# Linear attention and a gated mixture of experts on one core: batch 3's x^T by DMA transposes, 17 more zero matmuls, and another written order

## The chip, the cores and the metric

The kernel runs on one core of a Trainium2 chip. The metric is the device time of one execution in microseconds (us). Five engines work beside each other, each with its own instruction queue: PE (TensorE, matrix products), ACT (ScalarE, activations), DVE (VectorE, elementwise work), POOL (GpSimd) and SP (SyncE, which here only issues DMA transfers). Every engine takes its instructions strictly in the order in which they were written. An instruction that waits therefore holds up everything written behind it on its engine. The transfers themselves run on 16 DMA engines that all queues share.

## The reference

For 8 batches of 8 heads, with 576 tokens and a head dimension of 64, the kernel computes linear attention and then, with the 8 heads laid side by side (512 channels), one expert per token.

```python
phi = lambda x: np.where(x > 0, x, np.exp(x) - 1.0) + 1.0
kv = einsum('bhsd,bhse->bhde', phi(k), v);  z = sum(phi(k), axis=2)
x = einsum('bhsd,bhde->bhse', phi(q), kv) / (einsum('bhsd,bhd->bhs', phi(q), z)[..., None] + 1e-06)
...
logits = x @ w_gate;  local = sigmoid(x @ w_local)
# per token: the expert of the largest logit if local < 0.5 (or it is the first token), else the expert before
out[b, s] = p[e] * (relu(x[b, s] @ w1[e]) @ w2[e])
```

Here p is the softmax of the logits, w1 is 8 x 512 x 1024 and w2 is 8 x 1024 x 512.

## The kernel before, in words

The kernel assumes that one expert serves a whole batch, the one of its first token. It computes that case and a flag that says whether it held; only if it did not, a general branch follows (it isn't entered with these inputs).

The work is cut into 803 named steps. The list `ops` (lines 660 to 817) says for each step which engine takes it, what it needs, and which PSUM slot it takes or gives back. There are four PSUM slots of two banks each. `TURNS` (lines 92 to 131) is a permutation of the 803 steps, and the instructions are emitted in exactly that order; so it fixes the order on every engine and every DMA queue. The costs and latencies in `ops` are what a planner outside the kernel worked with; inside the kernel only the needs and the slots count. `fills` (line 88) says how many matmuls of zeros (`work`, line 825) PE does just ahead of a named step.

In the text n counts half batches (four heads each, 0 to 15), a counts batches (0 to 7), j = n mod 2, and h counts the two halves of a batch's first 512 tokens. The steps are:

- **Loads, SP queue.** Lk.n, Lv.n, Lq.n bring k, v and q of a half batch (`load`, `load_wide`, lines 154 to 196). Lk.n and Lv.n from n = 2 on are three DMA instructions each (L167 once, L170 twice), Lq.n is one (L159). There are 4 buffers for k, 3 for v and 2 for q, so Lk.n needs K.(n-4), Lv.n needs VC.(n-3), and Lq.n needs the DVE step P.q.(n-2). HOLD (line 542) is a tiny transfer that makes the loads of batches 2 to 7 wait until batch 0's w1 has landed. Lwg brings the gate weights.
- **phi, ACT and DVE.** E (exp, L279) and E2 (relu, L285) run on ACT, P.k.n (L307) and P.q.n (L314, two instructions) on DVE. VC.n copies v beside a column of ones (L326).
- **Attention, PE.** K.n accumulates kv (L337, L342; L349 for batch 0), KC.n copies it out (DVE, L354). Q.n and QL.a transpose phi(q) (L360, L374), QC.n and QLC.a copy that out (ACT, L366, L380). N.a.j.h and NL.a are the numerators and denominators (L401, L420); D.a.j.h and DL.a divide (DVE, L386, L388, L389) and write x in bf16 into `xb` (one buffer for each h, reused by every batch).
- **x transposed.** XL.a and XLC.a do the last 64 tokens on PE and DVE (L453, L457). For the other 512 tokens there are two ways. For batches a < TB, X.a.h is 8 PE transposes (`x_main`, L435) and XC.a.h a DVE copy (`x_main_out`, L440). For the others, X.a.h is two DMA transposes on the SP queue (`x_dma`, line 444, L447), 128 x 512 bf16 each, and XC.a.h stands for their landing.
- **Gate.** R.a.0 and R.a.1 are the logits (L468, L474), PK.a picks the expert of the first token (DVE), W.a.x issues the load of that expert's w1 or w2 on the POOL queue (L533, L536, L538; skipped by a condition if one of three slots holds it), CW.a.x copies it into the working buffer (DVE, L552). S1, S2, S3 make the gate's factor.
- **Experts.** H.a.m (m = 0 to 7) are 8 matmuls each for the hidden layer (L590); HC.a.m is the relu on ACT (L597). O.a.i (i = 0 to 4; O0 is the first part of O.a.0) is the output layer (L609, L613); OC.a.i scales it on ACT (L623, L625), and ST.a.* stores it (SP queue).

A need that matters below: D.a.j.h overwrites `xb`, so it needs the transposes of batch a-1 to have read it. In line 734 that is X.(a-1).h while a <= TB, and the landing XC.(a-1).h for a > TB. H.a.0 needs XC.a.0, XC.a.1, XLC.a and the expert's weights.

Of the kernel before, what the change touches and what calls it, by code (L numbers as in the profile page):

```python
# [48 lines left out]
def kernel(  # L49
# [28 lines left out]
    W = Dh + 1  # L78
    rows = [P, P, P, P, PH]
    LEAD = 2  # L80
    TB = 4
    NS = 3
    NX = 3
    BOTH = "kq"
    SLOTS = [2, 2, 2, 2]


    fills = {("FILL",): 19, ("QL", 0): 2, ("NL", 0): 2, ("XL", 0): 4, ("R", 0, 0): 2}

    TURNS = [
# [38 lines left out]
    ]  # L131

    consts = ctx.enter_context(tc.tile_pool(name="consts", bufs=1))
# [7 lines left out]
    with ExitStack() as main:  # L141
# [265 lines left out]
        def num_main_out(a, j, h):  # L407
            ps = open_.pop(("N", a, j, h))
            if (a, h) not in xb:
                xb[a, h] = xbp.tile([P, 2, NJ, 2, P], BF16, name=f"xb{h}")  # L410
            divide(ps[:, :, :4 * W].rearrange("p g (m w) -> p g m w", w=W), 4,
                   xb[a, h][:, :, j].rearrange("p i g (t e) -> p g i t e", t=2))
# [249 lines left out]
        def op(name, eng, length, rank, needs, fn, takes=None, gives=None):  # L662
            ops.append((name, [d for d in needs if d], takes, gives))
            run[name] = fn
# [9 lines left out]
        for a in range(B):  # L674
# [3 lines left out]
            for j in range(NJ):  # L678
# [51 lines left out]
                for h in range(2):  # L730
                    op(("N", a, j, h), "PE", 0.52, r + 2 + 3 * h - head, [("KC", n), ("QC", n)],
                       lambda a=a, j=j, h=h: num_main(a, j, h), takes=("a", 2))
                    op(("D", a, j, h), "DVE", 1.07, r - 3 + 3 * h - head,
                       [("N", a, j, h), a and ("XC" if a > TB else "X", a - 1, h)],
                       lambda a=a, j=j, h=h: num_main_out(a, j, h), gives=("N", a, j, h))
# [9 lines left out]
            for h in range(2):  # L745
                cs = [NC - 1] if h == 0 else list(range(NC - 1))
                if a < TB:
                    op(("X", a, h), "PE", 0.5, at + 6 + 4 * h - head, [("D", a, 0, h), ("D", a, 1, h)],
# [326 lines left out]
```

## Time and profile before

| what | value |
|---|---|
| median of 3 runs (lowest to highest) | 231.51 us (231.4 to 232.65) |
| the profiled execution's own time | 231.31 us |
| its span, first to last instruction | 229.6 us |
| PE busy | 208.6 us (91%) |
| ACT busy | 154.8 us (67%) |
| DVE busy | 148.6 us (65%) |
| matmuls of zeros (L827) | 8.8 us of PE |
| mean granted TensorE clock | 0.963 |
| DMA traffic | 48.83 MB |

The time lies 1.71 us over the span. The span falls in three stretches. Up to 39.83 us there is attention alone (batches 0 and 1). Then attention of the next batches and the experts of earlier ones are interleaved. From about 175 us on, only expert work is left. Stretches of the profile are given in us from the span's start.

### The profile page before, as it was taken

The numbers are of one execution on the slowest core, as the hardware profiler recorded it, in microseconds if no ns is written. First come the engines' busy times: TensorE is split into PE (matmuls) and PEld (weight loads), VectorE is DVE, ScalarE is ACT, GpSimd is POOL, SyncE is SP. The second block draws the span as 40 slices with busy tenths as digits, with TensorE's granted clock in tenths as the row PEclk, the third lists the DMA queues.
The fourth block names the chain that finished last, engine by engine and source line by source line (L and its number), as shares of the span: only waits on it lengthen the run. The fifth ranks groups of instructions, "written<-read, shape, count | busy, mean of one in ns | idle before, by whom it ended". The sixth has DMA issues, their size and how long they took to land.

```text
span 229.6 us, 7679 instructions
## 1 busy us (share of the span) xinstructions
PE 208.6 (91%) x3186; PEld 149.9 (65%) x3199; DVE 148.6 (65%) x420; ACT 154.8 (67%) x226; POOL 12.6 (5%) x41
## 2 busy tenths in 40 slices
PE   7688469899999999999999699999999999999990
PEld 2375368674888856988568486588657747647640
DVE  2756885778899989999997596996456264112000
ACT  3846933499999998998793979625534644636540
POOL 4002200000000000010002000101000011000000
PEclk9959959999999999999999999999999999999997
DMA  5998999973789897989999978699904759915132
GB/s 206 382 250 275 249 204 312 346 217 106 224 265 268 287 361 213 302 243 209 383 250 227 260 191 223 127 212 230 157 17 56 253 92 275 163 24 209 25 134 82
DMA packets 48076, 48.83 MB, mean 213 GB/s; under 512 B 19602, under 2 KB 40082, under 8 KB 47138
## 3 DMA queue, kind: packets, MB, share of 16 engines
q1 hardware_dynamic: 40850, 39.68, 58.9%
q0 software_dynamic: 6832, 8.45, 22.6%
q8 instruction: 27, 0.44, 0.8%
q10 hardware_dynamic: 352, 0.13, 0.2%
q14 instruction: 15, 0.12, 0.2%
HBM read 61.88 MB, written 9.44 MB: 311 GB/s over the span
## 4 chain that ended last, share of the span: by engine, by line
PE 78%; DMA 9%; DVE 3%; issue 2%; ACT 2%; SPq 2%; DVEq 1%
PE hps L590 26%; PE yps L609 23%; DMA vraw<-in_v_dram 6%; PE kvps L337 6%; PE tq L360 6%; PE nps L401 5%; PE yps L613 3%; DMA qraw<-in_q_dram 3%; PE kvps L342 2%; PE lps L474 1%; PE tx L435 1%; SPq L159 1%; PE npl L420 1%; PE kvps L349 1%; PE fill L827 1%
## 5 line engine op out<-in xcount | busy, mean ns | idle before, releaser
L590 PE MATMUL hps<-xT,w1cur 128*128 128x288 bf16 x512 | 66.7, 286 | 3.2 <-ACT hT L597 2.0
L590 PEld LDWEIGHTS <-w1cur 128*128 128x128 bf16 x512 | 48.4, 98 | 16.7 <-issue 4.5
L609 PE MATMUL yps<-w2cur,hT 128*128 128x512 bf16 x244 | 57.0, 379 | 1.1 <-DVE lt_all L479 0.5
L597 ACT ACTIVATE hT<-hps 128x576 bf16<-128x576 f32 x64 | 40.6, 649 | 23.8 <-PE hps L590 23.5
L609 PEld LDWEIGHTS <-hT 128*128 128x128 bf16 x256 | 24.3, 98 | 27.6 <-issue 0.4
L623 ACT ACTIVATE yo<-yps,pr 128x512 f32<-128x512 f32 x32 | 21.6, 694 | 20.0 <-PE yps L609 19.0
L389 DVE TENSOR_TENSOR xb<-nps,rec 128x512 bf16<-128x512 f32 x32 | 22.1, 691 | 2.9 <-DMA xT<-xb 1.8
L314 DVE SCALAR_TENSOR_TENSOR fq<-fq,qraw 128x576 f32<-128x576 f32 (+1 forms) x32 | 22.6, 742 | 0.8 <-ACT qraw L285 0.8
L279 ACT ACTIVATE fq<-qraw 128x1152 f32<-128x1152 f32 (+1 forms) x16 | 18.4, 1159 | 5.0 <-DMA qraw<-in_q_dram 5.0
L366 ACT COPY qT<-tq 128x512 f32<-128x512 f32 x32 | 18.1, 659 | 4.4 <-PE tq L360 4.4
L401 PE MATMUL nps<-kv,qT 64*64 64x65 f32 x1024 | 19.7, 220 | 0.6 <-ACT qT L366 0.6
L279 ACT ACTIVATE ek<-kraw 128x1152 f32<-128x1152 f32 x16 | 18.8, 1173 | 2.1 <-DMA kraw<-in_k_dram 2.1
L360 PE MATMUL tq<-ident,fq 128*128 128x128 f32 x128 | 18.9, 302 | 0.4 <-DVE lt_all L479 0.4
L401 PEld LDWEIGHTS nps<-kv,qT 64*64 64x64 f32 x1024 | 17.1, 134 | 2.9 <-ACT qT L366 0.7
L285 ACT ACTIVATE qraw<-qraw 128x1152 f32<-128x1152 f32 (+1 forms) x16 | 18.6, 1162 | 0.3
L307 DVE SCALAR_TENSOR_TENSOR kraw<-ek,kraw 128x1152 f32<-128x1152 f32 x14 | 18.7, 1346 | 0.0
L360 PEld LDWEIGHTS tq<-ident,fq 128*128 128x128 f32 x128 | 16.5, 157 | 0.8 <-issue 0.4
L285 ACT ACTIVATE kraw<-kraw 128x1152 f32<-128x1152 f32 x14 | 16.5, 1176 | 0.1
L337 PE MATMUL kvps<-vone,kraw 128*64 128x65 f32 x448 | 16.2, 224 | 0.0
L337 PEld LDWEIGHTS kvps<-vone,kraw 128*64 128x64 f32 x448 | 14.2, 137 | 2.3 <-issue 1.3
L552 DVE COPY w2cur<-w2s 128x4096 bf16 x7 | 8.5, 1220 | 9.6 <-PE yps L613 9.4
L552 DVE COPY w1cur<-w1s 128x4096 bf16 x7 | 8.6, 1226 | 6.7 <-PE hps L590 4.6
(97 smaller groups left out, 184.7 us busy)
## 6 DMA issues: line engine op xcount, KB each, us to landing
qraw<-in_q_dram SPq DMA_DIRECT2D x14, 576.0 KB, 5.8
kraw<-in_k_dram SPq DMA_DIRECT2D x14, 512.0 KB, 5.9
vraw<-in_v_dram SPq DMA_DIRECT2D x14, 512.0 KB, 5.6
w1s<-in_moe_w_dram POOLq DMA_DIRECT2D x7, 1024.0 KB, 9.3
w2s<-in_moe_w_dram POOLq DMA_DIRECT2D x7, 1024.0 KB, 12.6
out_dram<-yo SPq DMA_DIRECT2D x14, 512.0 KB, 5.2
kraw<-in_k_dram SPq DMA_DIRECT2D x2, 576.0 KB, 4.1
vraw<-in_v_dram SPq DMA_DIRECT2D x2, 576.0 KB, 8.0
```

Source lines behind the costliest of these rows:

```text
L279: nc.scalar.activation(e[:, :, c0:c1, :], raw_, Act.Exp)
L285: nc.scalar.activation(raw_, raw_, Act.Relu)
L307: nc.vector.scalar_tensor_tensor(r, e, 1.0, r, Alu.min, Alu.add)
L314: nc.vector.scalar_tensor_tensor(e[:, g], e[:, g], 1.0, r[:, g], Alu.min, Alu.add)
L337: nc.tensor.matmul(ps[g * PH:(g + 1) * PH, t, :W], lhsT=f[:, i, :], rhs=vo[:, i, :], start=(c == 0), stop=False)
L360: nc.tensor.transpose(ps[:, r, i * P:(i + 1) * P], ex_[n, "q"][:, 1 + i + (NC - 1) * r, :, :], identity=ident)
L389: nc.vector.tensor_tensor(dst, ps[:, :, :, :Dh].rearrange("p g (i t) e -> p g i t e", t=2), rec.rearrange("p g (i t o) -> p g i t o", t=2, ...
L401: nc.tensor.matmul(ps[o * PH:(o + 1) * PH, g, (il * 2 + t) * W:(il * 2 + t + 1) * W], lhsT=qT[n][g * PH:(g + 1) * PH, t, i * P + o * PH:i ...
L590: nc.tensor.matmul(ps[:, u, :HS], lhsT=w1b[:, kk, m * P:(m + 1) * P], rhs=xT[b][:, kk, u * HS:(u + 1) * HS], start=(kk == 0), stop=(kk == ...
L597: nc.scalar.activation(hT[b][:, m, :].rearrange("p (u s) -> p u s", u=2), open_.pop(("H", b, m))[:, :, :HS], Act.Relu)
L609: nc.tensor.matmul(ps, lhsT=hT[b][:, m, i * P:(i + 1) * P], rhs=w2b[:, m, :], start=(m == 0), stop=(m == FK - 1))
L623: nc.scalar.activation(ym[:, i, :], ps, Act.Copy, scale=pr[:, i:i + 1])
```

## The change

Three things are changed, and nothing else in the file. `TB` goes from 4 to 3, so that batch 3's X.3.0 and X.3.1 become four DMA transposes on the SP queue in place of 16 PE transposes and two DVE copies; at the same time D.4.j.h comes to need XC.3.h, the landing. `fills` has 46 zero matmuls in place of 29, which is 17 more by the diff (the change's own short description says 25 more). `TURNS` is another permutation.

```diff
-    TB = 4
+    TB = 3
...
-    fills = {("FILL",): 19, ("QL", 0): 2, ("NL", 0): 2, ("XL", 0): 4, ("R", 0, 0): 2}
+    fills = {("FILL",): 20, ("QL", 0): 2, ("K", 0): 3, ("K", 1): 3, ("NL", 0): 3, ("XL", 0): 4, ("R", 0, 0): 2,
+             ("N", 0, 1, 0): 3, ("N", 0, 1, 1): 2, ("X", 0, 0): 2, ("X", 0, 1): 2}
...
     TURNS = [
-        0, 8, 801, 25, 1, 2, 3, 28, 7, 5, 9, 30, 15, 4, 6, 10, 47, 29, 31, 26, 37, 16, 17, 38, 39, 11, 12, 13,
...
+        0, 25, 8, 801, 3, 1, 28, 9, 5, 30, 15, 16, 4, 10, 47, 48, 26, 37, 2, 7, 11, 27, 104, 798, 125, 32, 12,
...
```

Read as names, the parts of the two orders that the text below speaks of are these (the rest is left out):

```
SP, before: Lk.0 Lk.1 Lv.0 Lq.0 Lv.1 Lq.1 Lwg Lk.2 Lv.2 Lq.2 Lk.3 Lq.3 Lv.3 HOLD ...
SP, after:  Lk.0 Lk.1 Lv.0 Lv.1 Lq.0 Lq.1 Lk.2 Lwg Lk.3 Lv.2 Lq.2 Lv.3 Lq.3 HOLD Lq.4 Lk.4 Lv.4 ...
SP, before: ... Lk.14 ST.1.4 Lq.12 ST.1.0 Lv.14 X.4.0 Lq.13 X.4.1 Lk.15 Lq.14 ST.2.4 X.5.1 Lq.15 ...
SP, after:  ... Lk.13 Lq.11 X.3.0 X.3.1 Lk.14 Lq.12 Lk.15 Lv.14 ST.1.0 Lv.15 ST.1.4 Lq.13 X.4.0 Lq.14 X.4.1 Lq.15 ...

PE, before: ... X.0.1 X.0.0 R.0.1 Q.2 QL.1 Q.3 K.2 K.3 N.1.0.0 N.1.0.1 NL.1 N.1.1.0 H.0.0 H.0.1 ...
PE, after:  ... K.2 X.0.1 X.0.0 Q.2 QL.1 Q.3 R.0.1 H.0.0 N.1.0.0 K.3 N.1.0.1 NL.1 H.0.1 H.0.2 XL.1 H.0.3 N.1.1.1 H.0.4 R.1.0 N.1.1.0 ...
PE, between H.0.0 and H.2.0: only before X.3.0, R.2.1; only after N.1.0.0, K.3, N.1.0.1, NL.1, N.1.1.0, K.10, K.11, N.4.0.0, N.4.0.1
PE, from H.2.0 to the end:   only before X.3.1, K.10, K.11, N.4.0.0, N.4.0.1; only after R.2.1

ACT, before: ... QC.0 E.k.2 QC.1 E.q.2 E2.q.2 E.k.3 E2.k.3 E.q.3 E2.q.3 E2.k.2 QLC.1 QC.2 QC.3 ...
ACT, after:  ... E.k.2 QC.0 E2.k.2 E.k.3 E2.k.3 QC.1 E.q.2 E2.q.2 E.q.3 E2.q.3 QLC.1 QC.2 QC.3 HC.0.0 ...
ACT, between HC.0.4 and HC.2.0: only after E.k.12, E2.k.12, E2.q.10, E.q.11, E.k.13, E2.k.13, OC.1.4; only before none

DVE, before: ... VC.2 D.0.0.1 BK.0 D.0.1.0 D.0.0.0 D.0.1.1 P.q.2 XC.0.1 VC.3 XC.0.0 P.q.3 ...
DVE, after:  ... P.k.2 D.0.0.0 D.0.0.1 VC.2 D.0.1.1 D.0.1.0 P.q.2 P.q.3 KC.2 XC.0.1 XC.0.0 VC.3 P.k.3 ...
DVE, after:  ... D.3.0.0 CW.2.0 D.3.1.1 PK.3 KC.10 P.k.11 VC.11 P.k.12 P.q.10 D.4.0.0 KC.11 VC.12 D.4.0.1 ...
```

The order of the POOL queue (W.0.0 to W.7.1) is the same in both.

74 rows, old and new, of the table TURNS are left out of this document.

## Prediction

> **What bounds the kernel now.** I read the page first: the busy table, and the chain of waits followed back from the end.
>
> ```profile
> PE 208.6 (91%) x3186; PEld 149.9 (65%) x3199; DVE 148.6 (65%) x420; ACT 154.8 (67%) x226; POOL 12.6 (5%) x41
> L827 PE MATMUL fill<-zero 128*128 128x512 bf16 x28 | 8.8, 468 | 1.7 <-DVE warm L204 1.3 <-issue 0.3
> ```
>
> PE is busy 91% of the span, and what it isn't busy is 21.0 us (229.6 - 208.6). The busy time holds 8.8 us of zeros. The stretches of 10 us say where the idle time lies and which other engine is full there (columns: PE, PEld, DVE, ACT, POOL busy, granted clock, DMA share, GB/s).
>
> ```profile
> 20.00:30.00 10.00, 4.57 (x152) 3.81 (x152) 8.08 (x23) 8.70 (x10) 2.41 (x3) 0.92 1.04 226
> 30.00:40.00 10.00, 9.05 (x228) 8.38 (x229) 7.17 (x17) 3.01 (x8) 0.18 (x1) 0.74 1.18 264
> 50.00:60.00 10.00, 9.95 (x82) 6.25 (x81) 8.83 (x18) 9.94 (x15) 0.05 (x1) 1.00 0.57 169
> 70.00:80.00 10.00, 10.00 (x150) 8.51 (x147) 9.76 (x24) 9.87 (x19) 0.04 (x1) 1.00 0.92 285
> 90.00:100.00 10.00, 10.00 (x171) 8.44 (x170) 9.26 (x28) 9.65 (x15) 0.12 (x1) 1.00 0.90 280
> 120.00:130.00 10.00, 8.03 (x169) 6.41 (x168) 6.20 (x15) 5.79 (x9) 1.50 (x4) 1.00 1.27 217
> 220.00:229.60 9.60, 3.72 (x29) 1.85 (x27) 0.00 (x0) 1.85 (x3) 0.00 (x0) 0.83 0.37 129
> ```
>
> From 20 to 30 us PE has only 4.57 us of work. From 50 to 100 us it is never short of work, but ACT is 9.65 to 9.94 and DVE 8.83 to 9.76 of 10 beside it: **three engines are nearly full at once**. At 120 to 130 us PE loses 1.97 us, and ACT is down to 5.79. The end, after the last matmul, is fixed (the last stores). The chain in order of time gives three stations.
>
> ```profile
> 39.83 1.63 PE hps L590 x12
> ...
> 96.99 3.05 PE hps L590 x24
> ...
> 120.03 6.53 DMA qraw<-in_q_dram
> ...
> 222.73 1.01 PE yps L613 x16
> ```
>
> H.0.0, the first expert matmul, starts at 39.83. H.2.0 starts at 96.99. PE ends at 223.74; behind it lie 5.86 us to the end of the span, and 1.71 us from there to the execution's 231.31. The sum is made against that, 0.2 under the median of 231.51.
>
> **Part 1, the start.** What holds H.0.0 at 39.83 shows in the timeline of the first 40 us.
>
> ```profile
> 9.59 1.28 PE L349 MATMUL kvps<-vone,kraw 64*64 64x65 f32 x72 [0.81 <-ACT vone L324]
> 12.06 2.23 PE L349 MATMUL kvps<-vone,kraw 64*64 64x65 f32 x72 [1.19 <-DVE vone L326]
> 20.45 0.47 SPq L167 DMA_DIRECT2D vraw<-in_v_dram  x1
> 21.75 1.52 POOL L533 DMA_DIRECT2D w1cur<-in_moe_w_dram  x2 [18.23 <-DVE vone L326]
> 29.36 0.76 DVE L326 COPY vone<-vraw 128x1152 f32<-128x1152 f32 x1 [1.06 <-DMA vraw<-in_v_dram]
> 30.04 0.68 DVE L440 COPY xT<-tx 128x1024 bf16<-128x1024 bf16 x1
> 31.73 0.74 SPq L544 DMA_DIRECT2D there<-w1cur  x1
> ```
>
> The weights of batch 0 are issued at 21.75, and HOLD passes at 31.73: 10.0 us. x^T is complete at 30.72 (30.04 + 0.68), late because DVE stands at VC.3 for a v that SP issued only at 20.45, behind Lq.3. So both inputs of H.0.0 are there by 32, and the 8 us to 39.83 are other PE work written ahead of it, half of it at a halved clock:
>
> ```profile
> 11.00:12.00 1.00, 0.00 (x0) 0.00 (x0) 0.75 (x2) 1.00 (x3) 0.00 (x0) 0.69 1.05 361
> 29.00:30.00 1.00, 0.00 (x0) 0.00 (x0) 0.64 (x1) 1.00 (x2) 0.00 (x0) 0.50 1.26 208
> 34.00:35.00 1.00, 1.00 (x7) 0.90 (x5) 0.59 (x1) 1.00 (x3) 0.00 (x0) 0.50 1.24 205
> 35.00:36.00 1.00, 1.00 (x28) 0.77 (x28) 0.00 (x0) 0.77 (x3) 0.00 (x0) 0.86 1.19 252
> ```
>
> The new order has Lv.3 ahead of Lq.3, XC.0.1 and XC.0.0 ahead of VC.3 on DVE, Q.2, Q.3 and K.2 in PE's gap before H.0.0, and K.3 and three N behind it. What is late next is ACT: the two XC stand behind P.q.3, and that behind E2.q.3. E2.q.3 ends at 29.09 now (its row, behind this fence, 27.93 + 1.16); v.1 ahead of q.0 puts q about 1.4 us later (0.52 MB at the 361 GB/s of the row at 11 us), but K.1 falls from 2.23 to the 1.28 of K.0 at full clock, and QC.0 and QC.1 wait less for Q.0 and Q.1.
>
> ```profile
> 27.93 1.16 ACT L285 ACTIVATE qraw<-qraw 128x1152 f32<-128x1152 f32 x1
> ```
>
> I take E2.q.3 at 27, then P.q.3 1.4, KC.2 0.2, two copies of 0.68: x^T at 30. W.0.0 comes out at about 20, and with the same 10.0 us the weights are there by 30. **H.0.0 at 30.5**, 9.3 us earlier; bounds 29 and 34 (by 34, W.0.0 gains nothing and the waits at 31.73 stay). The 17 zeros cost nothing where PE waits anyway (20 to 30 us: 5.43 idle); if that cover is gone, 17 at about 0.21 us (12 loads of zeros took 2.47 us at speed) are 3.6 us. The upper bound 34 holds that.
>
> The clock fell at 11 us though PE had done work in every microsecond before. The Trainium skill, "TensorE: Matmul & The Clock Gate", Part 1, says that one idle window of about 3.4 us brings half rate; here a window only part filled did it, so zeros in short gaps can matter. The same page, Part 4, says that transposes don't count as activity for the gate, which would speak against Q.2 and Q.3 as cover. The trace disagrees: from 31 to 35 us PE did almost only transposes (Q.2, QL.1, Q.3), and the mean clock of the microsecond from 35 is 0.86, on the way up. By that rule H.0.0's first 3 to 4 us would run at half rate, about 2 us more.
>
> **Part 2, from H.0.0 to H.2.0.** Here the new order does more attention than the old one. Costs of a step, one contiguous piece of the chain and the ACT row:
>
> ```profile
> 100.03 0.45 PE tx L435 x8
> 100.48 0.39 PE npl L420 x16
> 100.87 0.47 PE nps L401 x32
> 101.34 1.08 PE kvps L337 x32
> 102.43 0.28 PE kvps L342 x8
> ...
> L279 ACT ACTIVATE ek<-kraw 128x1152 f32<-128x1152 f32 x16 | 18.8, 1173 | 2.1 <-DMA kraw<-in_k_dram 2.1
> L474 PE MATMUL lps<-wg,xT 128*128 128x9 bf16 x128 | 4.4, 168 | 3.5 <-DVE xT L440 3.5
> ```
>
> PE gains three K (1.36 each), five N (0.47) and NL.1 (0.3), and loses X.3.0 (0.45) and R.2.1 (0.4): 4.1 + 2.35 + 0.3 - 0.85 = +5.9 us. Now H.0.0 to H.2.0 takes 57.2 us, of which 1.3 are idle; so PE alone would need 61.8 and reach H.2.0 at 92.3. But **ACT is full here**. From HC.0.4 to HC.2.0 it takes
>
> ```profile
> 46.10 0.65 ACT L597 ACTIVATE hT<-hps 128x576 bf16<-128x576 f32 x1 [0.33 <-PE hps L590]
> 98.70 0.63 ACT L597 ACTIVATE hT<-hps 128x576 bf16<-128x576 f32 x1
> ```
>
> 52.6 us with hardly a gap, and six E or E2 (1.16 each) and OC.1.4 (about 0.4) are added: 59.9 us. H.0.4 ends 8.2 us after H.0.0 (five H of 0.98, K.3, four steps N or NL, XL.1), so HC.0.4 starts at 38.7, HC.2.0 at 98.6, and **H.2.0 at 97.3**: no earlier than now. DVE gains a net of about 4 us in the same stretch and is as full. The head start of 9.3 us is thus paid out as work done sooner, with ACT as the engine that sets the pace; bounds 93 (PE's sum) and 101 (ACT and DVE waiting 3 us more for loads that now have to come sooner). DMA stands at a share of 0.57 to 0.92 there, so the loads can come sooner, and HOLD passes about 2 us earlier.
>
> **Part 3, from H.2.0 to the end.** PE has 126.75 us from 96.99 to 223.74, with 2.6 us idle (1.97 of it in the row at 120). It loses X.3.1 (0.45), K.10 and K.11 (2.72) and two N (0.94) and gains R.2.1 (0.4): 124.15 - 3.7 = 120.45 us.
>
> **Part 4, batch 3's transposes.** The DVE copies (0.68 each) go. In their place SP issues four DMA transposes between Lq.11 and Lk.14, and D.4.j.h waits for their landing. Of before, batch 4's and 5's show what that costs:
>
> ```profile
> 114.46 5.45 SPq L447 DMA_TRANSPOSE xT<-xb  x2
> 120.60 3.45 SPq L447 DMA_TRANSPOSE xT<-xb  x2
> xT<-xb SPq DMA_TRANSPOSE x2, 8.6
> xT<-xb SPq DMA_TRANSPOSE x6, 5.0
> DVE xb L389 <- DMA xT<-xb: 1.8, 1, 1.8
> ACT fq L279 <- DMA qraw<-in_q_dram: 5.0, 3, 3.9
> ```
>
> A pair holds SP 3.5 to 5.5 us under load and lands 5.0 to 8.6 us after its issue; D.5 then waited 1.8 us on DVE, and ACT 3.9 us for the q that had stood behind the first pair on SP. In the new order DVE reaches D.4.0.0 about 6 us after D.3.1.1 (PK.3, KC.10, P.k.11, VC.11, P.k.12, P.q.10), and D.4.0.1 2 us later. X.3.0's pair lands about then, X.3.1's pair 1 to 5 us late. Behind them on SP stand Lk.14, Lq.12, Lk.15 and Lv.14; E.k.14 and E.q.12 are wanted after HC.2.4, about 4 us after they can be issued. DVE is full, so I take 2 us of PE idle here and 1 us for the later transposes: 3 us in place of 2.6. Bounds: 0.5 (they land in time) and 9 (5 here, and the 3.9 again).
>
> The sum: 97.3 + 120.45 + 3.0 = 220.75 for PE's end; with 5.86 the span is 226.6, with 1.71 the time is **228.3 us**, 1.3% under 231.31.
>
> The Trainium skill, "DMA: Bandwidth & Descriptors", Latency and other measured facts, gives DMA transposes 261 GB/s, by which 128 KB would take an estimated 0.5 us; the landing of 5.0 to 8.6 us here is queueing behind loads, so by that figure alone D.4 would not wait and the sum would be 2 us lower.
>
> **The rivals.** (a) *The head start is kept*: ACT's added steps fit gaps, H.2.0 is at PE's own sum and a little, 93.5, and 2 us are idle later: 93.5 + 120.45 + 2 + 7.57 = 223.5. For it: ACT has 0.06 to 0.35 us of gaps in the rows of 10 us above, and its waits for PE would vanish. Against it: such gaps make 1 to 2 us of 50, not 4. (b) *The start doesn't move enough*: Lwg now stands behind Lk.2 on SP, and WG on DVE ahead of XLC.0; if the gate weights or the q loads are late, H.0.0 is at 34 and all behind ACT shifts by 3.5: 231.8, no change. The same case holds a clock that falls again before H.0.0, as at 29 us now, so that its first 4 us run at half rate: 2 us more. That is what Part 4 of the Trainium skill's page "TensorE: Matmul & The Clock Gate" would lead to. (c) *Slower*: X.3 on SP and DVE. If X.3.0's pair lands 8.6 us after issue behind loads, D.4.0.0 and D.4.0.1 wait 5 us, and the loads behind on SP starve ACT by the 3.9 us of before once more: 9 us in place of 3, 234.3. It decides once the second pair lands more than about 5 us after DVE wants it, at a stretch in which neither ACT nor DVE can catch up. That the transposes don't take place as said can be left aside; line 747 is a plain comparison with TB.
>
> **How the numbers follow.** Forecast case (ACT sets the pace, 3 us idle): 0.38, 226 to 230.3. Head start kept: 0.20, about 223.5. No change: 0.14. Slower: 0.28, 233 to 236. A measurement of this kernel can tell about 0.5% from no change (1.2 us). So faster 0.58, same 0.14, slower 0.28. The range leaves out a tenth on each side: 222.8 to 234.8, which takes in the start's bounds (29 and 34: -1.5 and +3.5), ACT's (93: -4.3) and the transposes' (+6).
>
> **What would show it.** Right: the first L590 near 30.5; granted clock 1.00 from 11 to 35 us; ACT at 9.7 or more of 10 from 45 to 95; the L590 of batch 2 near 97; a wait of DVE's L389 for DMA xT of 1 to 3 us near 95. Wrong: H.0.0 after 34, or PE without idle from 45 to 95 (then (a)), or waits of ACT on q and k loads over 5 us in all behind X.3 (then (c)).

## The result, and the profile after

| | before | after |
|---|---|---|
| median (lowest to highest), same chip | 232.08 us (231.4 to 236.09) | 240.2 us (239.62 to 241.96) |
| ratio, 95% interval | | 1.04 [1.031, 1.049] |
| the profiled execution's own time, span | 231.31, 229.6 us | 240.12, 238.5 us |

The changed kernel is 4% slower; 228.3 us with a range up to 234.8 was forecast. (Ratios here and below are formed from the executions that lie within 1.5% of the fastest of their kernel, so a ratio can differ a little from that of the medians.) Lines of code behind L88 stand one line later than in the kernel before: L591 is H, L598 is HC, L448 the DMA transposes.

The chain of waits in order of time, cut to a few lines, gives the stations that the prediction named.

```profile
20.28 9.15 DMA qraw<-in_q_dram
29.45 1.17 ACT fq L280
...
31.84 0.07 DVE fq L315
...
36.50 1.94 PE hps L591 x8
...
100.71 9.38 DMA xT<-xb
...
118.38 11.44 DMA qraw<-in_q_dram
...
231.05 1.01 PE yps L614 x16
```

H.0.0 starts at 36.5 us in place of 30.5, behind a load of q that took 9.15 us. H.2.0 starts at 104.16 in place of 97.3, PE ends at 232.06 in place of 220.75. The stretches of 10 us (columns as before) say where PE had nothing to do.

```profile
20.00:30.00 10.00, 6.95 (x139) 4.97 (x139) 6.74 (x16) 5.05 (x7) 2.41 (x3) 1.00 1.07 258
30.00:40.00 10.00, 6.47 (x78) 4.98 (x80) 5.27 (x10) 5.06 (x9) 0.18 (x1) 0.66 1.19 267
50.00:60.00 10.00, 9.58 (x96) 6.19 (x97) 9.42 (x16) 9.94 (x12) 0.04 (x1) 1.00 0.88 272
70.00:80.00 10.00, 10.00 (x165) 8.30 (x161) 9.62 (x34) 9.84 (x16) 0.04 (x1) 1.00 0.82 246
90.00:100.00 10.00, 9.88 (x150) 6.43 (x151) 9.69 (x25) 8.93 (x12) 0.23 (x1) 1.00 1.02 265
100.00:110.00 10.00, 6.94 (x145) 5.50 (x145) 4.30 (x10) 8.99 (x14) 0.54 (x1) 1.00 1.13 180
120.00:130.00 10.00, 9.65 (x166) 6.87 (x167) 8.12 (x32) 5.75 (x12) 0.19 (x2) 1.00 1.24 243
130.00:140.00 10.00, 8.62 (x176) 6.25 (x175) 7.92 (x20) 9.33 (x14) 0.03 (x1) 1.00 0.87 177
```

Two places lose: 20 to 40 us (6.6 us idle, and the clock at 0.66 in the second row) and 100 to 110 us (3.1 us). In the second, DMA moves only 180 GB/s at a share of 1.13. The timeline shows who waited at the start.

```profile
20.19 1.52 POOL L534 DMA_DIRECT2D w1cur<-in_moe_w_dram  x2 [16.67 <-DVE tag L490]
20.28 1.17 SPq L160 DMA_DIRECT2D qraw<-in_q_dram  x1
29.45 1.16 ACT L280 ACTIVATE fq<-qraw 128x1152 f32<-128x1152 f32 x1 [3.50 <-DMA qraw<-in_q_dram]
31.84 1.43 DVE L315 SCALAR_TENSOR_TENSOR fq<-fq,qraw 128x576 f32<-128x576 f32 x2 [4.43 <-ACT qraw L286]
32.25 0.73 SPq L545 DMA_DIRECT2D there<-w1cur  x1
33.39 1.28 DVE L441 COPY xT<-tx 128x1024 bf16<-128x1024 bf16 x2
33.53 0.69 PE L375 MATMUL tql<-ident,fq 128*128 128x128 f32 x2 [4.87 <-DVE kv L355]
```

The weights of batch 0 are issued at 20.19, as forecast. But Lq.3 is issued at the same moment, behind Lv.3, and shares the DMA engines with them. ACT waits 3.5 us for q.3, DVE 4.4 us for ACT at P.q.3, and the two copies of x^T stand behind P.q.3. PE waits 4.9 us, its clock falls, and H.0.0's eight matmuls take 1.94 us. The clock in the first microsecond of the work that follows, and in the one in which it comes back:

```profile
33.00:34.00 1.00, 0.47 (x2) 0.29 (x2) 1.00 (x4) 0.00 (x0) 0.00 (x0) 0.50 1.24 208
39.00:40.00 1.00, 1.00 (x32) 0.88 (x27) 0.37 (x2) 0.13 (x1) 0.00 (x0) 0.59 1.15 320
```

At X.3 the waits are these.

```profile
95.86 6.11 SPq L448 DMA_TRANSPOSE xT<-xb  x4
99.78 0.77 POOL L539 DMA_DIRECT2D w1s<-in_moe_w_dram  x1 [18.21 <-DVE vone L327]
110.22 0.69 DVE L390 TENSOR_TENSOR xb<-nps,rec 128x512 bf16<-128x512 f32 x1 [4.62 <-DMA xT<-xb]
110.96 3.52 PE L591 MATMUL hps<-xT,w1cur 128*128 128x288 bf16 x16 [3.69 <-DVE xb L390]
```

D.4.0.1 waits 4.62 us on DVE for X.3.1's landing, and with it all that DVE and then PE do. In the middle of X.3's issuing POOL issues W.3.0, the 1 MB of batch 3's w1 (its expert is in none of the three slots, so it is loaded). The prediction did not look at W.3.0 at all.

### The profile page after: what moved, and what is told of

Read it like the earlier page. It is cut to its first block, busy times and chain, and to the rows that moved or that the text cites. A ratio compares the mean times of both kernels' runs of the same rounds, so it can differ in the third digit from the quotient of the medians.

```text
span 238.5 us, 7698 instructions
## 1 busy us (share of the span) xinstructions
PE 214.6 (90%) x3180; PEld 150.3 (63%) x3200; DVE 146.8 (62%) x418; ACT 155.4 (65%) x226; POOL 11.6 (5%) x41
## 2 busy tenths in 40 slices
DMA packets 50252, 49.35 MB, mean 207 GB/s; under 512 B 21778, under 2 KB 42258, under 8 KB 49314
## 4 chain that ended last, share of the span: by engine, by line
PE 58%; DMA 21%; ACT 10%; DVE 3%; issue 3%; SPq 2%; DVEq 0%; ACTq 0%
PE hps L591 23%; PE yps L610 17%; DMA qraw<-in_q_dram 14%; PE nps L402 4%; DMA xT<-xb 4%; PE tq L361 4%; PE yps L614 3%; PE kvps L338 3%; ACT fq L280 3%; ACT ek L280 2%; DMA vraw<-in_v_dram 2%; ACT qraw L286 2%; DVE kraw L308 1%; SPq L160 1%; DMA kraw<-in_k_dram 1%
## 5 line engine op out<-in xcount | busy, mean ns | idle before, releaser
L591 PE MATMUL hps<-xT,w1cur 128*128 128x288 bf16 x512 | 69.4, 292 | 4.3 <-DVE xb L390 3.7
L598 ACT ACTIVATE hT<-hps 128x576 bf16<-128x576 f32 x64 | 40.9, 650 | 32.1 <-PE hps L591 32.0
L591 PEld LDWEIGHTS <-w1cur 128*128 128x128 bf16 x512 | 49.3, 99 | 18.8 <-issue 5.5
L402 PE MATMUL nps<-kv,qT 64*64 64x65 f32 x1024 | 21.3, 225 | 2.3 <-ACT qT L367 2.3
L402 PEld LDWEIGHTS nps<-kv,qT 64*64 64x64 f32 x1024 | 17.9, 137 | 6.7 <-ACT qT L367 3.3
L361 PE MATMUL tq<-ident,fq 128*128 128x128 f32 x128 | 17.6, 285 | 0.1
L361 PEld LDWEIGHTS tq<-ident,fq 128*128 128x128 f32 x128 | 14.6, 146 | 1.3 <-issue 0.5
```

Source lines behind the costliest of these rows:

```text
L361: nc.tensor.transpose(ps[:, r, i * P:(i + 1) * P], ex_[n, "q"][:, 1 + i + (NC - 1) * r, :, :], identity=ident)
L402: nc.tensor.matmul(ps[o * PH:(o + 1) * PH, g, (il * 2 + t) * W:(il * 2 + t + 1) * W], lhsT=qT[n][g * PH:(g + 1) * PH, t, i * P + o * PH:i ...
L591: nc.tensor.matmul(ps[:, u, :HS], lhsT=w1b[:, kk, m * P:(m + 1) * P], rhs=xT[b][:, kk, u * HS:(u + 1) * HS], start=(kk == 0), stop=(kk == ...
L598: nc.scalar.activation(hT[b][:, m, :].rearrange("p (u s) -> p u s", u=2), open_.pop(("H", b, m))[:, :, :HS], Act.Relu)
```

## The experiments

My theory after this reading: two separate losses, (1) q.3, loaded last before the weights and beside them, sets H.0.0; (2) X.3's transposes, slow beside W.3.0, hold D.4.0.1. The rivals are that the new written order loses by itself, that the zeros cost time, that the transposes are slow whatever is beside them, and that batch 3's weights cost every order the same. Each group of kernels was run on one chip together with the kernel before, and every ratio is to that.

**The start.** The first kernel is the changed one with one move on SP; the second is the changed one with the old zeros.

```diff
 SP:
-... Lq.2 Lv.3 Lq.3 HOLD ...
+... Lq.2 Lq.3 Lv.3 HOLD ...
```

> The changed kernel with one step moved: Lq.3 ahead of Lv.3 on the SP queue, so that q of half batch 3 is issued at about 18.4 us in place of 20.3, ahead of batch 0's weights (issued at 20.2). Theory: q.3 landed at 29.45 because it stood in the transfers behind v.3 and beside the weights; it then lands by about 25, ACT's E.q.3 starts by 26, x^T is complete by 31 in place of 34.7, PE has no gap of 5 us, the clock stays up, and H.0.0 starts at 31 to 33 in place of 36.5; ACT's pace from HC.0.4 on is unchanged, so the time falls by 3.5 to 6 us, to 234 to 237 us. Rival: the weights of batch 0 take the DMA engines whichever comes first, or x^T is then held by v.3, and H.0.0 stays at 36 or later: 239 to 241 us.

```diff
-    fills = {("FILL",): 20, ("QL", 0): 2, ("K", 0): 3, ("K", 1): 3, ("NL", 0): 3, ("XL", 0): 4, ("R", 0, 0): 2,
-             ("N", 0, 1, 0): 3, ("N", 0, 1, 1): 2, ("X", 0, 0): 2, ("X", 0, 1): 2}
+    fills = {("FILL",): 19, ("QL", 0): 2, ("NL", 0): 2, ("XL", 0): 4, ("R", 0, 0): 2}
```

> The changed kernel with the 29 zero matmuls of before in place of 46. Theory: the added zeros keep the clock at 1.00 from 8 to 28 us but the start waits for q.3's landing at 29.45 all the same, so H.0.0 and the time are within 1 us of the changed kernel (239 to 241 us), with a granted clock of 0.5 between about 12 and 18 us. Rival: the zeros carry the start (without them H.0.0 later than 38, 242 us or more), or they delay it (H.0.0 before 35.5, 239 us or less).

With q.3 first: 236.77 us, ratio 1.035 [1.022, 1.049]. The rows of the stretches of 10 us:

```profile
30.00:40.00 10.00, 9.84 (x218) 8.16 (x217) 8.77 (x27) 5.26 (x11) 0.18 (x1) 1.00 1.16 275
100.00:110.00 10.00, 5.13 (x34) 3.31 (x35) 4.49 (x8) 4.59 (x7) 0.20 (x1) 0.83 1.17 245
```

H.0.0 comes at 31.75, and 30 to 40 us is full at full clock: the start is settled as forecast once q.3 is not last. But the time hardly moves. D.4.0.1's wait grows from 4.6 to 6.1 us, and the stretch from 100 us has PE at 5.13 in place of 6.94. With the old zeros: 237.49 us, 1.037 [1.027, 1.046], the same as with the new ones within the intervals. But here I had expected H.0.0 to stay, and its rival came out: H.0.0 is at 32.4 without the move. The last transpose of X.3 took 9.95 us at 94.7, so this gain too was lost later. The start of that kernel:

```profile
20.14 0.54 SPq L159 DMA_DIRECT2D qraw<-in_q_dram  x1
20.93 1.52 POOL L533 DMA_DIRECT2D w1cur<-in_moe_w_dram  x2 [17.41 <-DVE tag L489]
26.42 1.17 ACT L279 ACTIVATE fq<-qraw 128x1152 f32<-128x1152 f32 x1 [1.46 <-DMA qraw<-in_q_dram]
```

SP issues q.3 here 0.8 us ahead of batch 0's weights, and ACT has it at 26.42. In the changed kernel, and in the four other kernels below that keep its start, q.3 is issued 0.1 to 1.9 us behind the weights; ACT has it at 29.3 to 31.5 us, and H.0.0 starts at 36.2 to 38.4. In the four kernels with Lq.3 moved ahead, H.0.0 starts at 31.75 to 32.4. So q.3 was late wherever it was issued beside the weights or behind them, and a lead of 0.8 us was enough to spare it. That the old zeros brought this lead about, by W.0.0 coming out later (20.93 in place of 20.19), rests on one profiled execution. The zeros cost no time that can be told.

**The transposes, with and without the new order.** One kernel is the changed one with X.3 on PE again (X.3.0 behind K.10, X.3.1 behind Q.9, the copies behind KC.10 and P.k.11). The other is the kernel before with the opposite edit alone.

```diff
-    TB = 3
+    TB = 4
```

> The changed kernel with TB back at 4: batch 3's x^T by 16 PE transposes (after K.10 and after Q.9) and two DVE copies (after KC.10) in place of the four DMA transposes on SP; D.4 no longer waits for a landing. Theory: the wait of 4.6 us on DVE at 105.6 us, the 3.7 us of PE idle behind it and the halved clock after that go, and the loads behind X.3 on SP come sooner; the PE and DVE work comes back (0.9 and 1.2 us): the time falls by 3 to 5 us, to 235 to 237 us. Rival: the new order itself sets the pace there through ACT and late loads, and the gap only moves: within 1.5 us of 240.

```diff
-    TB = 4
+    TB = 3
```

> The kernel before with TB = 3 alone, its own written order kept (on SP X.3.0 then stands between Lq.11 and Lk.13, X.3.1 between Lk.13 and Lv.13). Theory that the transposes cost what they cost beside loads: D.4 waits for their landing on DVE for 2 to 5 us and the loads behind them come 4 to 8 us later: 233.5 to 237 us. Rival: the transposes are harmless or a gain by themselves (0.9 us of PE and 1.2 us of DVE less) and only the new order makes them late: 230.5 to 232 us.

X.3 on PE: 236.08 us, 1.020 [1.000, 1.039], although H.0.0 came at 38.4 there; the stretch from 100 us is full (first fence, from an execution of 237.52 us). TB = 3 in the old order: 234.95 us, 1.023 [1.010, 1.035], and the same stretch loses 4.9 us (second fence).

```profile
100.00:110.00 10.00, 9.95 (x169) 7.56 (x168) 9.86 (x16) 9.97 (x15) 1.23 (x2) 1.00 1.08 265
```

```profile
100.00:110.00 10.00, 5.14 (x73) 3.98 (x75) 6.40 (x14) 4.90 (x8) 0.88 (x1) 0.96 1.18 232
```

So batch 3's transposes by DMA cost about 2% in either order; in the new one the intervals of 1.040 and 1.020 still overlap, and the pair with q.3 first, 1.035 here and 1.011 [1.006, 1.017] further down, is the clearer one. In the old order the one that waits is not D.4 but ACT, 5.1 us for k.14, which took 9.39 us at 98.61: the price is paid by whatever is due then.

**What makes the landing late.** Either W.3.0 beside it, or the loads ahead on SP, or the transposes themselves. The first edit takes batch 3's load away, in the changed kernel and, as a control, in the kernel before: batch 3 then uses an expert that is already in a slot, so its outputs are another expert's. The second moves two loads behind X.3.

```diff
-            nc.vector.max_with_indices(m8, i8, lt_all[0:1, b, NC - 1, :E])
+            nc.vector.max_with_indices(m8, i8, lt_all[0:1, 0 if b == 3 else b, NC - 1, :E])
```

> The changed kernel, but batch 3's expert is chosen from batch 0's logits, so that it is found in a slot and its 2 MB aren't loaded (the outputs of batch 3 are those of another expert; a later batch that wants batch 3's own expert may load it then). It tests whether W.3.0's transfer (issued at 99.9 us) makes X.3.1's transposes land late. Theory A (W.3.0 shares the DMA engines with the transposes): the last transpose of x^T lands in about 6 us in place of 9.4, D.4.0.1's wait falls from 4.6 us to 1 to 2, the stage from 100 to 110 us has TensorE busy about 9 us in place of 6.9, and the time falls by 3 us, to about 237. Theory B (the transposes are slow by themselves and behind the loads issued before them on the same queue): the wait stays at 4 to 5 us and the time within 1 us of the changed kernel's.

> The control of the fifth experiment: the kernel before, with batch 3's expert chosen from batch 0's logits, so that its 2 MB aren't loaded then (the outputs of batch 3 are those of another expert, and batch 4 loads the one that batch 3 wanted). In the profile of the kernel before W.3.0 is issued at 99.9 us and W.3.1 at 108.5, with no transpose on the way before 114 us, and ScalarE waits 3.9 us for q.14 at 120 to 130 us. If the weights of batch 3 cost mainly where transposes are beside them: the time falls by 0 to 3 us (ratio 0.987 to 1.0), far less than the 8 us that the same edit takes from the changed kernel. If the weights of batch 3 cost any order the same: it falls by 6 us or more (ratio 0.975 or below), and the fifth experiment says nothing of the transposes.

```diff
 SP:
-... Lk.13 Lq.11 X.3.0 X.3.1 Lk.14 ...
+... X.3.0 X.3.1 Lk.13 Lq.11 Lk.14 ...
```

> The changed kernel, but the loads Lk.13 and Lq.11, which SP issues just before X.3, come just behind X.3.1. It tests whether the loads ahead of the transposes on SP's queue make them land late. If they do: the last transpose lands in 5 to 6 us, D.4.0.1 waits 0 to 1.5 us in place of 4.6, but k.13 and q.11 are issued about 8 us later (102 us in place of 93 to 95), land at 110 or after, and ScalarE waits for them 3 to 5 us in the same stage: time 238 to 241, no better. If the loads ahead do not matter: D.4.0.1 still waits 4 to 5 us, ScalarE waits too, and the time rises by 2 us or more, to 242 and over.

Without W.3 the changed kernel takes 231.86 us, 0.996 [0.991, 1.002]: about 8 us less than with it, more than Theory A expected. The kernel before gains nothing that can be told: 230.02 us, 0.996 [0.990, 1.002]. So the weights alone are not the price; the weights together with X.3's transposes are.

The 2 MB are not gone, though. Batch 4 wants the same expert; it finds it in a slot in the changed kernel, but has to load it here, and both kernels move 49.35 MB:

```profile
124.13 0.77 POOL L539 DMA_DIRECT2D w1s<-in_moe_w_dram  x1 [15.70 <-DVE xb L390]
```

W.4.1 follows at 133.60, and PE is busy 9.90 and 9.76 us of the rows from 120 and 130 us. So the experiment moves the weights by 21 to 24 us, to a place where they cost next to nothing. Batch 3 itself can't use that place: its first product starts at 123.25 in the kernel before.

Here are the rows of the changed kernel's tile xT from 94 to 105 us, first with W.3.0 beside X.3, then without it; the last row of each gives the time from issue to landing:

```profile
L448 SPq DMA_TRANSPOSE xT<-xb x4: 1212/1290/2112, 95.9 to 100.7; - x4
...
  DVE xb L390: 4.6, 1
...
DMA to landing us min/median/max: 4.8/6.1/9.4
```

```profile
L448 SPq DMA_TRANSPOSE xT<-xb x4: 1213/1290/2000, 96.1 to 100.9; - x4
...
  DVE xb L390: 0.2, 1
...
DMA to landing us min/median/max: 3.4/5.6/6.1
```

The transposes are issued at the same moments in both, and the slowest takes 3.3 us less to land; nobody waits for it longer than 0.2 us. And without W.3 the stretch from 100 us is full:

```profile
100.00:110.00 10.00, 10.00 (x205) 7.97 (x204) 9.27 (x17) 9.97 (x16) 1.00 (x3) 1.00 0.96 219
```

From H.2.0 to PE's end the kernel then takes 120.9 us (103.84 to 224.7) in place of 127.9. The control takes 126.7 (94.30 to 221.04), and the kernel before 126.8.

X.3 ahead of two loads: 242.52 us, 1.047 [1.037, 1.056]. The transposes landed within 2.9 to 4.8 us and D.4.0.1 no longer waited, as expected for loads that matter. But it was worse in all: ACT waited 9.1 us at a stretch for q.11. What is moved behind four transposes is late itself. Nor does this run show that the two loads were the cause: with them out of the way, the last transpose was issued 1.0 us ahead of W.3.0 (98.89 and 99.93) in place of 0.9 us behind it (100.71 and 99.78). In the new order the slowest landing of X.3 took 9.4 to 11.0 us in the three kernels that issued W.3.0 before the last transpose (the changed one, q.3 first, the old zeros), and at most 6.2 in the five that did not (this one, and the two without W.3 and the two with W.3.0 late of this text). In the old order with TB = 3 it took 6.2 us even behind W.3.0; there k.14 was late.

**Moving W.3.0 instead.** If the load may not lie beside X.3, it can come later: PK.3, which picks the expert, is written behind D.4.0.1 (in the old order, with TB = 3, behind CW.2.1 together with BK.3).

```diff
 DVE:
-... D.3.1.1 PK.3 KC.10 P.k.11 VC.11 P.k.12 P.q.10 D.4.0.0 KC.11 VC.12 D.4.0.1 ...
+... D.3.1.1 KC.10 P.k.11 VC.11 P.k.12 P.q.10 D.4.0.0 KC.11 VC.12 D.4.0.1 PK.3 ...
```

> The changed kernel, but the choice of batch 3's expert (PK.3 on VectorE) and with it the load W.3.0 come behind D.4.0.1, so that 1 MB of weights is issued at about 107 to 110 us in place of 99.8, when x^T of batch 3 has landed. Nothing is left out. Theory A (W.3.0 beside X.3.1 makes the loss of that stage): D.4.0.1 waits under 1 us in place of 4.6, the stage from 100 to 110 us has TensorE busy 9.5 us or more, and the time falls by 4 to 8 us, to 232 to 236. Theory B (W.3.0 hurts what is transferred beside it wherever it stands): D.4.0.1 no longer waits, but q.12, k.15 or x^T of batch 4 land 4 us or more later, the idle time appears at 115 to 135 us, and the time is 238 to 241.

> The kernel before with TB = 3 as in the third experiment (batch 3's x^T by DMA in the old written order, which was 2.3% slower), and PK.3, BK.3 and W.3.0 behind CW.2.1 on VectorE, so that W.3.0 is issued at about 107 us in place of 96.8. Theory A (the loss by TB = 3 is the collision with W.3.0): k.14 lands in 5 to 6 us in place of 9.4, ScalarE waits for it under 1.5 us in place of 5.1, and the time is equal to or below that of the kernel before (ratio 0.985 to 1.005). Theory B (the transposes cost that by themselves): ratio 1.015 to 1.035 again.

> Both moves on the changed kernel: Lq.3 ahead of Lv.3, and PK.3 with W.3.0 behind D.4.0.1. Both terms of the prediction that failed are then given their conditions: H.0.0 at 31 to 32 us, batch 2's first product at 97 to 99, no idle time over 1.5 us at X.3. If the sum of the prediction is right in its other terms, the time is 227 to 230, ratio 0.975 to 0.995. If the head start is given back where ScalarE or the DMA queues are full, or the collision moves on: 232 to 237.

Theory B of the first of these held, and the time came out above even its range: 242.61 us, 1.059 [1.049, 1.070]. The stretches of 10 us and the waits from 85 to 140 us of that kernel:

```profile
100.00:110.00 10.00, 10.00 (x237) 8.32 (x230) 8.51 (x25) 9.85 (x13) 1.65 (x2) 1.00 0.94 254
110.00:120.00 10.00, 9.95 (x132) 7.31 (x133) 7.81 (x27) 7.84 (x15) 0.00 (x0) 1.00 1.10 277
120.00:130.00 10.00, 3.72 (x99) 2.36 (x96) 3.23 (x16) 1.37 (x2) 0.18 (x1) 0.79 1.22 222
```

```profile
ACT fq L280 <- DMA qraw<-in_q_dram: 8.6, 1, 8.6
...
DVE xb L390 <- DMA xT<-xb: 5.9, 1, 5.9
```

X.3 is clean now, and the stretch from 100 us is full. But W.3.0 (107.71) and W.3.1 (108.63) come together, X.4 runs beside both, and x^T of batch 4 and q.13 are late: 6.3 us of PE idle in one row. With q.3 first as well it is 238.67 us, 1.039 [1.025, 1.052], with PE at 2.17 from 120 us. The old order with TB = 3 and W.3.0 late: 237.34 us, 1.036 [1.025, 1.048], no better than without the move. So 8 to 11 us later is no better place: the weights then meet X.4. Of the places tried, only that behind 124 us was free, where batch 3 can't use it. An earlier one, ahead of X.3, was not tried.

**The whole sum, and a better version.**

> The changed kernel with both suspects taken out: Lq.3 ahead of Lv.3 on SP, and batch 3's x^T made on TensorE again (TB = 4, X.3.0 behind K.10 and X.3.1 behind Q.9). What is left of the change is the zeros and the rest of the new written order. If the loss of 8 us is these two alone (late q.3 about 4.5 us, the stage at 100 to 110 us about 4 us): H.0.0 at 31 to 33 us, batch 2's first product at 98 to 99, that stage without an idle time of TensorE over 1.5 us, and a time of 228.5 to 231.5, equal to the kernel before (ratio 0.99 to 1.005). If the new order loses somewhere else too, or if the head start is given back to a full ScalarE: 232.5 to 236.

> The changed kernel with Lq.3 ahead of Lv.3 and with batch 3's weights not loaded (its outputs are those of another expert): both terms of the prediction that failed have their conditions, and the collision has no place to move to. If those two terms are the whole error: H.0.0 at 31 to 33 us, batch 2's first product at 97 to 99, no idle time over 1.5 us from 95 to 120 us, and 225 to 229 us (the 228.3 of the forecast or below), ratio 0.97 to 0.99. If a third loss is hidden (the head start given back, a later queue): 230 to 234.

> The kernel before with two moves and nothing else: on SP, Lv.3 ahead of Lq.3; on VectorE, XC.0.0 ahead of VC.3. It is the first experiment turned round, for the kernel before, where the load issued last before the weights is v.3. If what is loaded last by SP before the weights sets H.0.0 whatever it is, q.3 becomes late in turn: H.0.0 does not move from 37 to 38 us or comes later, and the time is 231 to 234. If the weights alone set H.0.0 in the kernel before, XC.0.0 comes 2 to 3 us earlier, H.0.0 about 1 us, and the time is 229.5 to 231.

> The kernel before with everything that the runs so far speak for: Lv.3 ahead of Lq.3 and VC.3 behind XC.0.0 (ratio 0.9865 alone), batch 3's x^T by DMA (TB = 3), and W.3.0 behind CW.2.1. If the transposes are worth the 2.6 us of TensorE that they take away, and W.3.0 is out of their way: ratio 0.975 to 0.985, below the one with the two moves alone. If TB = 3 is worth nothing even so: 0.985 to 0.995. If it still collides with something: over 1.

The edits are those above: the new order with q.3 first and X.3 on PE; the changed kernel with q.3 first and without W.3 (outputs of batch 3 again from another expert). The last two start from the kernel before, with these two moves on SP and DVE; the last adds TB = 3 and the late W.3.0:

```diff
 SP:
-... Lk.3 Lq.3 Lv.3 HOLD ...
+... Lk.3 Lv.3 Lq.3 HOLD ...
 DVE:
-... XC.0.1 VC.3 XC.0.0 P.q.3 ...
+... XC.0.1 XC.0.0 VC.3 P.q.3 ...
```

The new order with q.3 first and X.3 on PE takes 232.24 us, 1.011 [1.006, 1.017], above the 0.99 to 1.005 that I expected if these two were the whole loss. With q.3 first and no W.3 it is 230.22 us, 1.003 [0.998, 1.007]: not the 225 to 229 expected there. A third loss shows in the row of 90 us of the second kernel and in ACT's waits from 45 to 100 us:

```profile
90.00:100.00 10.00, 7.30 (x126) 5.26 (x116) 8.02 (x19) 7.60 (x12) 0.04 (x1) 1.00 1.03 277
```

```profile
ACT fq L280 <- DMA qraw<-in_q_dram: 4.3, 3, 2.1
```

From HC.0.4 to HC.2.0 that kernel takes 63.3 us (41.08 to 104.40). In the other kernels with Lq.3 moved ahead it is 61.4 (X.3 on PE), 61.5 (W.3.0 late) and 61.8 (the move alone). The changed kernel takes 59.4, without W.3 58.6, with W.3 late 58.4. Of the 5.5 to 6.3 us by which HC.0.4 comes earlier than in the changed kernel, 2 to 4 are given back; in the second kernel loads of q that land late between 45 and 100 us are part of it (4.3 us of ACT's waits). That is not a law: with the old zeros HC.0.4 was as early (41.91), and the same stretch took 58.4. Why the loads kept up there stays open.

The kernel before with its two moves takes 230.74 us, 0.987 [0.980, 0.993]: by this ratio 1.3% faster, but the medians of all executions (232.02 for the kernel before) are only 0.6% apart, so the size of the gain is open. Its cause is open too. In its profiled execution HC.0.0 starts at 39.66 (41.01 before) and H.0.0 at 38.5; but three kernels with the start of the kernel before unchanged had H.0.0 at 37.25 to 38.7, so the moves are not shown to have brought it. That execution, of 232.12 us, lost 2 us again at 120 to 130 us. Here q.3 is issued last too, but 1.7 us ahead of the weights, and ACT has it at 26.55: the last place alone did not make it late. With TB = 3 and W.3.0 late on top of it the time is 237.4 us, 1.030 [1.017, 1.043]. With W.3 loaded, the transposes of batch 3 cost about 2% or more in every order tried.

## Why the prediction was wrong

Its terms against the changed kernel, and against that with q.3 first and no W.3, in us:

| term | forecast | after | q.3 first, no W.3 |
|---|---|---|---|
| H.0.0 | 30.5 | 36.5 | 32.2 |
| H.0.0 to HC.0.4 | 8.2 | 10.3 | 8.9 |
| HC.0.4 to HC.2.0 | 59.9 | 59.4 | 63.3 |
| H.2.0 ahead of HC.2.0 | 1.3 | 2.1 | 2.1 |
| H.2.0 to PE's end | 120.45 + 3.0 | 127.9 | 120.3 |
| behind PE's end | 7.57 | 8.06 | 7.6 |
| time | 228.3 | 240.1 | 230.2 |

Two steps failed. Part 4's decides the time: with batch 3's weights out of X.3's way the changed kernel is 8 us faster. Part 1's is the larger term by itself, but mending it alone brings the ratio only from 1.040 to 1.035, since the gain is lost again behind it.

**Part 1 failed, by 6 us, and beyond its bound of 34.** W.0.0 came out at 20.19, as forecast. The step that failed is "I take E2.q.3 at 27"; it ended at 31.81. The step counted ACT's and DVE's work, and took Lv.3 ahead of Lq.3 as a gain for VC.3, without asking when q.3 would now be issued. The prediction's own reading (VC.3 late for a v that SP issued only at 20.45) was applied to v.3 in the old order and not to q.3 in the new one, which is issued at 20.28, beside the weights. The first experiment, one move, brought H.0.0 to 31.75. The weights were mis-sized as well, 12.1 us from issue to HOLD (20.19 to 32.25) in place of 10.0, but no trace shows H.0.0 waiting for them. A second part of it was the clock: the sum let H.0.0 follow at full clock, but behind the gap at 28.7 to 33.5 us the clock was at half until 39.8 us. With q.3 first, at full clock, the next term is 8.9 us, so about 1.4 of the 2.1 us by which it is over are the clock's. The rival (b) named this, "a clock that falls again before H.0.0", at 2 us, but only as part of a case that ended at 231.8. That the 17 zeros cost nothing is borne out as far as the time goes (1.037 without them, 1.040 with them).

**Part 2 was right in its size.** From HC.0.4 to HC.2.0 it took 59.4 us against 59.9. That ACT alone sets the pace is less sure: in these 59.4 us ACT was idle 1.5 and PE 1.9. PE's own sum was too low: between H.0.0 and H.2.0 it worked 65.2 us at full clock (q.3 first, no W.3) and not 61.8, so the two engines were nearly level. And the bound of "ACT and DVE waiting 3 us more for loads that now have to come sooner" was the usual case where the start was early: 61.4 to 63.3 us, with one exception.

**Part 3 was right.** In the kernel with q.3 first and no W.3, PE is never idle from H.2.0 on, and its work took 120.3 us against 120.45.

**Part 4 failed in its size:** all idle and slowed time behind H.2.0 is 7.45 us (127.9 - 120.45) in place of 3, inside the bound of 9. It priced the transposes from X.4 and X.5, "5.0 to 8.6 us after its issue", as queueing behind loads on SP. It left out that the 8.6 had W.3.1 beside it (issued at 108.52, 15.8 us to landing), and that X.3 would have W.3.0; batch 3's weights beside X.3 stood in the sum at nothing. Taking W.3 away brought the landing to at most 6.1 us, the wait to 0.2, and the time down by 8 us. The rival (c) named the first half of its nine rightly (D.4 waits 5 us; measured 4.62), but gave it to loads ahead on SP. The wait went with these loads in place once the weights were away, so they are not needed to explain it; what they add of themselves isn't separated. Its second half did not come: behind X.3 ACT waited 1.8 us for q, not 3.9.

The Trainium skill, "DMA: Bandwidth & Descriptors", Latency and other measured facts, gives DMA transposes 261 GB/s, and the prediction added that by this figure alone D.4 would not wait. No landing here comes near the 0.5 us estimated from it: without W.3 nobody waited, but the transposes still took 3.4 to 6.1 us to land.

**The range failed because its ends were taken as alternatives.** The late start (+3.5 at its bound) and the transposes (+6 at theirs) are of one kind, a transfer that something waits for beside 1 MB of weights, and they came together. Even added they give only 237.8, since the start went beyond its bound.

Even with both failed terms mended there was no gain: in the kernel with q.3 first and no W.3, the head start of 7.7 us (39.83 to 32.16) and the 6.5 us saved behind H.2.0 (120.3 against 126.8) were spent on 13 us more between H.0.0 and H.2.0 (70.1 against 57.1). The forecast gain of 3 us hung on that difference of large numbers.

## What to carry to other kernels

When an order of transfers is changed, ask of each load that is now issued beside a large one who waits for it (first it was v.3, then q.3). A small transfer that something waits for is at risk beside a large one on another queue: its place on its own queue did not protect q.3 or X.3 here, while a lead of 0.8 us ahead of the large one was enough for q.3 in one kernel. Moving the large one only helps if there is a stretch with room, and here only one 21 to 24 us later was shown to be free. Where two risks are of the same kind, add them in the range.

## What the runs showed of the hardware

While 1 MB of weights was on its way by POOL's queue, a load of k on SP's queue took about twice its time to land. The issues between 95 and 112 us, with W.3.0 and without it (KB of each, median us from issue to landing):

```profile
w1s<-in_moe_w_dram POOLq DMA_DIRECT2D x1, 1024.0 KB, 9.9
kraw<-in_k_dram SPq DMA_DIRECT2D x2, 512.0 KB, 9.1
```

```profile
kraw<-in_k_dram SPq DMA_DIRECT2D x2, 512.0 KB, 4.9
```

After a gap the clock stayed at half for 4.1 to 6.3 us of work: PE resumed at 33.53 us and had the full clock from about 39.8 in the changed kernel; without W.3 it resumed at 34.80 and had it from about 38.9. In both, the first 2.6 us of that work are transposes. The stretch at half clock itself was equally long in both, 6.8 us (from 33.0 and from 32.0), and as long in the kernel before (from 28.4). The 2 us between them are only how far it had run when PE resumed: 0.5 us in the one, 2.8 in the other. Whether the transposes shortened or lengthened it, these two traces don't tell.
